# A convolution by two-step transforms on one core: transfers of 48, 32, 64 and 16 rows, and the spectra in DRAM by frequency, then token

## The chip, the cores and the metric

The kernel runs on one core of one Trainium2 chip. The metric is the device time of one execution in microseconds (us). Three timed runs of the kernel before took 922.99, 924.22 and 924.59 us; the median is 924.22 us. The profile that is read below is one more execution, whose instructions span 914.5 us.

## The reference, cut to what matters

Two blocks follow each other. The first is a causal long convolution of each of 128 channels, over 5696 tokens, in 8 batches, with a filter h of the same length:

```python
Xf = np.fft.rfft(x, n=2*S, axis=1)          # x: (8, 5696, 128)
Hf = np.fft.rfft(h, n=2*S, axis=0)          # h: (5696, 128)
y  = np.fft.irfft(Xf * Hf[None], n=2*S, axis=1)[:, :S, :]
```

The second takes y as 45568 tokens of 128 numbers and is a mixture of experts with soft slots (phi: 128 x 32):

```python
logits = y @ phi                            # (45568, 32)
d = softmax(logits, over tokens)            # dispatch
slots = d.T @ y                             # 32 x 128, through 8 small networks w1, relu, w2
c = softmax(logits, over slots)             # combine
out = c @ slot_out                          # (45568, 128)
```

Everything is float32.

## The kernel before, in words

The tokens are laid out as a grid of R1 = 89 rows by N2 = 64 columns. A transform of length N = N1 N2 = 90 x 64 with half-shifted frequencies does the convolution in two steps: one over the rows (90 frequencies, of which pairs are kept as two halves of NP = 45), one over the columns (64). Between the steps the data has to change which index lies on the 128 partitions, and that is done by way of DRAM. So there are three stages, joined by two arrays in DRAM, `f` (the spectra after the first step) and `z` (the products after the second step, turned back over the columns):

- **Stage A** works on a *chunk*: CH = 4 columns and their 4 mirror columns of one input (the filter is input 0, the batches are 1 to 8; 8 chunks each, 72 in all). `load_x` brings the chunk into one of three tiles `xc`, rows on partitions. Before, it is two DMAs, of 80 rows and of 9 rows, to partitions 20 to 108 (`X0 = 20`), each row being two runs of 2 KB (L190). `fold` adds or subtracts the mirror columns on GpSimd (POOL, L201). `stage_a` multiplies by the table `s1` on TensorE (PE, L212), ScalarE (ACT) copies the two results into a tile `fst` (L214), and two DMAs (L218) store it: one for each half `a` of the frequencies, 45 rows each, from partitions 6 to 50 and 82 to 126 (`F0, F1 = 6, 82`). This happens twice a chunk (`comp`), so that a chunk has four stores of `f`.
- **Stage B** works on a *unit* of four frequencies of one input (12 units an input; the twelfth has one frequency). `load_g` loads it into one of three tiles `gt` (L236), now with the columns of both halves on 128 partitions. `stage_b1` multiplies by `wt` on PE (L250) and by the filter's spectrum on VectorE (DVE, L268 and L277); `stage_b2` multiplies by `vt` on PE (L292), ACT copies (L297), and one DMA stores `z` in runs of 1 KB (L300).
- **Stage C** works on a *pair* of chunks of `z`. `load_pair` (L328) loads it with 90 frequencies on partitions, as two DMAs given by `z_blocks`: 64 rows to partitions 32 to 95, and 26 rows to partitions 0 to 25, 16 KB a row. `stage_c1` multiplies by the table `i1` on PE (L347), and the rest turns the result and runs the softmaxes and the dispatch.

In DRAM, before, `f` of an input has the shape (2, 64, 45, 2, 128): half, column, frequency, real or imaginary, channel. A store of `f` therefore writes 4 runs of 1 KB from each of its 45 rows. A load of a unit reads, for each of 128 rows (half, column), one run of 4 KB, since four frequencies lie side by side.

Rows of a tile that no transfer writes are still read by the matmuls, which take all 128 partitions; so the kernel clears the three `xc` tiles and the `zc` tile on DVE at the start (L177, L314). In the tail a second tile `zd` takes the place of released memory, and its gap (partitions 26 to 31) is copied from `zc` by a DMA (L657) ahead of its first load.

The order of the work is written out by hand: a loop over steps t issues one chunk of stage A, one or two units of stage B behind it (1.5 on average), and every second step one pair of stage C. Nearly all DMAs are issued by SyncE (SP), one after another in program order. DMAs take turns on eight completion semaphores, and a DMA waits, on SP, until the one eight DMAs earlier has landed. So at most eight are under way, and a DMA that waits on SP holds all later ones. The buffers are: three `xc`, two folded `x`, five `fst`, three `gt` (loaded two units ahead), three `zst`.

Of the kernel before, what the change touches and what calls it, by code (L numbers as in the profile page):

```python
# [10 lines left out]
F32 = mybir.dt.float32  # L11
# [5 lines left out]

def z_blocks(n):

    return [(0, 64, 32), (64, n - 64, 0)]  # L20


def transform_tables(S, N1, N2, CH, X0, F0, F1):

    N, R1, HALF, P = N1 * N2, S // N2, N2 // 2, 2 * N2
    k1 = np.arange(N1)
    alpha = np.pi * (k1 + 0.5) / N1
    m1 = np.arange(R1) - (N1 - 1) / 2
    a1 = np.outer(m1, alpha)  # L40
    s1 = np.stack([np.cos(a1), -np.sin(a1), -np.cos(a1)], 1)
    a0 = np.outer(alpha, np.arange(N1 // 2) + 0.5)
    i1 = np.stack([np.cos(a0), -np.sin(a0), -np.cos(a0)], 1)
    NP = N1 // 2
    part = s1
    s1 = np.zeros((P, 3, P))
    for a, p in enumerate((F0, F1)):
        s1[X0:X0 + R1, :, p:p + NP] = part[:, :, a * NP:(a + 1) * NP]
    part = i1[np.arange(N1).reshape(2, NP).T.reshape(-1)]
    i1 = np.zeros((P, 3, N2))  # L50
    for r, n, p in z_blocks(N1):
        i1[p:p + n, :, 0:NP] = part[r:r + n]
    k2 = np.arange(N2)
    omega = np.pi * (k1[:, None] + 2 * N1 * k2[None] + 0.5) / N
    m2 = np.arange(HALF) - (N2 - 1) / 2
    a2 = m2[None, :, None] * omega[:, None, :]
    w = np.concatenate([np.cos(a2), np.sin(a2)], 1)
    back = np.arange(N2).reshape(2, HALF // CH, CH).transpose(1, 0, 2).reshape(-1)
    NU = (NP + 1) // 2
    turn = (N1 - 1) / 2 * alpha[:, None] + (N2 - 1) / 2 * omega  # L60
    wq = np.zeros((2, N2, NP, N2))
    vq = np.zeros((2, N2, NU, 2, N2))
    tn = np.zeros((2, N2, 2, (NU + 1) // 2, 2, 2))
    for a in range(2):
# [10 lines left out]
def kernel(  # L75
# [40 lines left out]
    HP = P // 2  # L116
    NQ = NJ // 2
    assert S == R1 * N2 and R1 == N1 - 1 and D == P and CH == Q == 4
    SPLIT = R1 // 16 * 16
    X0, F0, F1 = 20, 6, 82  # L120
    ctx.enter_context(tc.manual_schedule())

    t_s1, t_i1, t_w, t_v, t_turn = [
        nc.inline_tensor(t, f"tab_{n}").ap()
        for n, t in zip(("s1", "i1", "w", "v", "turn"), transform_tables(S, N1, N2, CH, X0, F0, F1))]
    fd = [nc.dram_tensor(f"f_{g}", (2, N2, NP, 2, D), F32, kind="Internal").ap() for g in range(B + 1)]
    zd = [nc.dram_tensor(f"z_{b}", (NP, 2 * N2, 2, D), F32, kind="Internal").ap() for b in range(B)]
    cd = nc.dram_tensor("c_t", (P, B * NQ, Q, 2, MH), F32, kind="Internal").ap()

# [43 lines left out]
    xs = {}  # L173
    xf = [apool.tile([P, CH, D], F32, name=f"x{i}", tag=f"x{i}", bufs=1) for i in range(2)]
    xcs = [apool.tile([P, 2, CH, D], F32, name=f"xc{i}", tag=f"xc{i}", bufs=1) for i in range(3)]
    for t_ in xcs:
        nc.vector.memset(t_[:, :, :, :], 0.0)  # L177

    def load_x(c):
        if c >= (B + 1) * NJ:  # L180
            return
        g, j = divmod(c, NJ)
        src = (h if g == 0 else x[g - 1]).rearrange("(a n) d -> a n d", n=N2)
        t_ = xcs[c % len(xcs)]
        gap = N2 - CH * (2 * j + 1)
        for r in (slice(0, SPLIT), slice(SPLIT, R1)):
            v = src[r, CH * j:CH * (j + 1), :]
            v = bass.AP(tensor=v.tensor, offset=v.offset,
                        ap=[v.ap[0], [gap * D, 2], [1, CH * D]])
            nc.sync.dma_start(  # L190
                out=t_[X0 + r.start:X0 + r.stop, :, :, :].rearrange("p s n d -> p s (n d)"), in_=v)
        xs[c] = t_

    folded = {}
# [1 line left out]
    def fold(c, comp):  # L196
        if c not in xs:
            return
        t_ = xs.pop(c) if comp else xs[c]
        y_ = xf[comp]  # L200
        nc.gpsimd.tensor_tensor(out=y_[:, :, :], in0=t_[:, 0, :, :], in1=t_[:, 1, ::-1, :],  # L201
                                op=AL.subtract if comp else AL.add)
        folded[(c, comp)] = y_

    def stage_a(c, comp):
        g, j = divmod(c, NJ)
        src = folded.pop((c, comp))
        tab = (0, 1) if comp == 0 else (1, 2)
        st = apool.tile([P, CH, 2, D], F32, name="fst", tag="fst", bufs=5)
        for G in range(2):  # L210
            p = bank()
            nc.tensor.matmul(p[:, :], s1[:, tab[G], :],  # L212
                             src[:, :, :].rearrange("p n d -> p (n d)"), start=True, stop=True)
            nc.scalar.activation(st[:, :, G, :],  # L214
                                 p[:, :].rearrange("p (n d) -> p n d", d=D), AF.Copy)
        n0 = comp * HALF + CH * j
        for a, p in enumerate((F0, F1)):
            nc.sync.dma_start(  # L218
                out=fd[g][a, n0:n0 + CH, :, :, :].rearrange("n q c d -> q n (c d)"),
                in_=st[p:p + NP, :, :, :].rearrange("k n c d -> k n (c d)"))  # L220


    gs, prods = {}, {}
# [6 lines left out]
    def load_g(u):  # L230
        if u >= (B + 1) * NW:
            return
        g, w, us = parts(u)
        n = sum(k for _, k in us)
        t_ = bpool.tile([P, 4, 2, D], F32, name="gt", tag="gt", bufs=3)
        nc.sync.dma_start(  # L236
            out=t_[:, 0:n, :, :].rearrange("p q c d -> p (q c d)"),
            in_=fd[g].rearrange("a r q c d -> (a r) (q c d)")[:, 8 * w * D:(8 * w + 2 * n) * D])
        gs[u] = t_

    def stage_b1(u, share):
# [62 lines left out]


    zs, ys, Ls, ds = {}, {}, {}, {}
    zn = used = None
    ybufs = [ypool.tile([P, Q * CH, D + 1], F32, name=f"y{i}") for i in range(2)]
    zring = [ypool.tile([P, 2, 2, CH, 2, D], F32, name="zc")]
    lt = ypool.tile([P, CH, 2, HP], F32, name="lt")  # L310
    dt = ypool.tile([P, CH, 2, HP], F32, name="dt")
    om, op = [ypool.tile([P, CH, D], F32, name=n) for n in ("om", "op")]
    yt = ypool.tile([D, Q * CH, 2, MH], F32, name="yt")
    nc.vector.memset(zring[0][:, :, :, :, :, :], 0.0)  # L314
    for t_ in (lt, dt):
        nc.vector.memset(t_[:, :, :, :], 0.0)
    for t_ in ybufs:
# [15 lines left out]

    def stage_c1(T, between):
        t_ = zs.pop(T)
        kr = used if t_ is zn else P
        y_ = ybufs.pop(0)
        ybufs.append(y_)

        def part(v, f):  # L340
            k = (2 * v + f) * CH
            return y_[:, k:k + CH, 0:D] if f == 0 else y_[:, k + CH - 1:k - 1:-1, 0:D]

        def product(o, tab, q):
            p = bank()
            for h_ in range(2):
                nc.tensor.matmul(p[h_ * HP:(h_ + 1) * HP, :], i1[0:kr, tab, :],  # L347
                                 t_[0:kr, h_, o, :, q, :], start=True, stop=True)
# [212 lines left out]
    for t in range(last_front + 1):  # L561
# [82 lines left out]
        if NA < t <= NA + E:  # L644
# [2 lines left out]


    T = V + 1
    (_, n0, p0), (_, n1, p1) = z_blocks(N1)  # L650
    gap, used = slice(p1 + n1, p0), p0 + n0
# [5 lines left out]
    nc.sync.dma_start(out=zn[gap, :, :, :, :, :].rearrange("k h o n c d -> k (h o n c d)"),  # L657
                      in_=zring[0][gap, :, :, :, :, :].rearrange("k h o n c d -> k (h o n c d)"))
    zring.insert(0, zn)
    load_pair(V + 2)  # L660
    nc.sync.dma_start(out=w1s[:, E - 1, :], in_=moe_w1[E - 1])
# [74 lines left out]
    p = bank()  # L736
# [127 lines left out]
```

## Time and profile before

| what | busy us of 914.5 | share |
|---|---|---|
| TensorE matmuls (PE) | 812.2 | 89% |
| VectorE (DVE) | 645.8 | 71% |
| ScalarE (ACT) | 481.1 | 53% |
| GpSimd (POOL) | 405.2 | 44% |
| the main DMA queue, mean of 16 engines | | 91.7% |

The core moves 272.43 MB, 142.86 MB read from and 128.21 MB written to its memory. The transfers concerned are:

| transfer | line | count | KB each |
|---|---|---|---|
| f <- fst | L218 | 288 | 180 |
| gt <- f | L236 | 99 and 9 | 512 and 128 |
| xc <- x, h | L190 | 72 and 72 | 320 and 36 |
| z <- zst | L300 | 88 and 8 | 512 and 128 |
| zc, zd <- z | L328 | 32 and 32 | 1024 and 416 |

How to read the profile: a group of instructions is named by its line in the kernel, its engine, its operation and the tiles it writes and reads. A wait is given as engine, line and tile, then an arrow, then who ended it; the numbers after it are us in total, how often, and the longest. PEld is TensorE's loading of weights; SPq, PEq and so on are the sequencers that issue. In the strips of 40 digits each digit is a slice of the span, in tenths busy. PEclk, and the number after POOL's in a table by stages, is the share of TensorE's clock that was granted. Beside the groups there are records of every DMA packet, with its start, its duration and its size, but not its direction.

### The profile page before, as it was taken

To read this page: it belongs to the slowest core of one execution; us is meant where nothing else is said; L and a number is where in the kernel's file an instruction comes from. 1 tells how busy PE (TensorE), PEld (TensorE's weight loads), DVE (VectorE), ACT (ScalarE), POOL (GpSimd) and SP (SyncE) were. 2 spreads that over 40 slices of the span, in tenths; PEclk is the share of its full clock that TensorE was granted. 3 is DMA by queue.
4 is the path that set the end of the run, shared out by engine and by line. 5 is a ranking of instruction groups with operands and counts; after the bars stand their busy time and mean duration, and the time that the engine had idled before them with its cause. 6 is when DMAs were issued, how large, how long until landed. Compare 5 with 4: busy or idle time off the path is not lost.

```text
span 914.5 us, 19226 instructions
## 1 busy us (share of the span) xinstructions
PE 812.2 (89%) x7220; PEld 425.9 (47%) x7220; DVE 645.8 (71%) x928; ACT 481.1 (53%) x888; POOL 405.2 (44%) x385
## 2 busy tenths in 40 slices
PE   6968888799999999999999999999988776978893
PEld 2323344344454444544555445444444443345783
DVE  3058767667888878877888777868888885774552
ACT  4624445456556565655666565555654344474442
POOL 4624333245555555555555555555533432472000
PEclk9989999999999999999999999999999998788865
DMA  9999899999999999999999999989989998751798
GB/s 302 269 282 310 256 326 347 292 323 340 285 324 331 304 281 323 320 329 280 329 323 317 289 317 313 311 281 325 334 266 338 305 295 206 223 220 74 281 404 340
DMA packets 156550, 272.43 MB, mean 298 GB/s; under 512 B 11766, under 2 KB 114422, under 8 KB 153317
## 3 DMA queue, kind: packets, MB, share of 16 engines
q1 hardware_dynamic: 155883, 270.85, 91.7%
q8 instruction: 58, 0.95, 0.4%
q10 hardware_dynamic: 576, 0.36, 0.2%
q14 instruction: 33, 0.27, 0.1%
HBM read 142.86 MB, written 128.21 MB: 296 GB/s over the span
## 4 chain that ended last, share of the span: by engine, by line
PE 61%; DMA 27%; issue 4%; ACT 2%; DVE 2%; POOL 2%; SPq 1%; DVEq 0%; POOLq 0%; ACTq 0%
PE bank L212 19%; PE bank L347 10%; PE bt L250 9%; DMA zc<-z 8%; PE bz L292 7%; DMA gt<-f 6%; DMA out_dram<-o 4%; PE bank L375 3%; PE bank L460 3%; DMA zd<-z 3%; DMA z<-zst 2%; DMA f<-fst 2%; PE bank L384 2%; PE bank L436 2%; PE op L817 1%
## 5 line engine op out<-in xcount | busy, mean ns | idle before, releaser
L201 POOL TENSOR_TENSOR x<-xc 128x512 f32<-128x512 f32 x144 | 183.1, 1273 | 260.5 <-PE bank L212 156.9
L212 PE MATMUL bank<-x,s 128*128 128x512 f32 x576 | 273.9, 611 | 9.7 <-POOL x L201 9.6
L214 ACT ACTIVATE fst<-bank 128x512 f32<-128x512 f32 x288 | 171.8, 597 | 94.7 <-PE bank L212 88.3
L297 ACT ACTIVATE zst<-bz 128x1024 f32<-128x1024 f32 x96 | 93.2, 971 | 195.2 <-PE bz L292 191.5
L268 DVE TENSOR_TENSOR p<-bt,Hi 128x1024 f32<-128x1024 f32 x96 | 113.0, 1177 | 107.3 <-PE bt L250 107.1
L212 PEld LDWEIGHTS bank<-x,s 128*128 128x128 f32 x576 | 102.1, 192 | 126.9 <-issue 94.1
L250 PE MATMUL bt<-gt,wt 64*64 64x256 f32 x1620 | 117.4, 397 | 40.0 <-DMA gt<-f 19.8
L347 PE MATMUL bank<-zc,i 128*64 128x512 f32 x480 | 118.0, 614 | 8.5 <-DMA zc<-z 6.2
L277 DVE TENSOR_TENSOR yf<-bt,p 128x512 f32<-128x512 f32 x192 | 119.4, 663 | 3.3
L268 DVE TENSOR_TENSOR bt<-bt,Hr 128x1024 f32<-128x1024 f32 x96 | 113.0, 1178 | 0.0
L250 PEld LDWEIGHTS bt<-gt,wt 64*64 64x64 f32 x1620 | 55.9, 134 | 117.0 <-issue 61.7
L292 PE MATMUL bz<-yf,vt 64*64 64x256 f32 x1440 | 103.7, 386 | 0.0
L366 POOL TENSOR_TENSOR y<-y,op 128x512 f32<-128x512 f32 x64 | 77.4, 1209 | 11.8 <-DVE op L352 9.1
L292 PEld LDWEIGHTS bz<-yf,vt 64*64 64x64 f32 x1440 | 61.8, 136 | 21.1
L366 POOL TENSOR_TENSOR y<-y,om 128x512 f32<-128x512 f32 x54 | 64.0, 1185 | 2.1
L347 PEld LDWEIGHTS bank<-zc,i 128*64 128x64 f32 x480 | 30.9, 138 | 70.3 <-issue 47.4
L375 PE MATMUL bank<-ident,y 109*128 109x109 f32 x512 | 57.5, 268 | 0.7 <-DVE y L366 0.7
L375 PEld LDWEIGHTS bank<-ident,y 109*128 109x128 f32 x512 | 51.2, 146 | 12.9 <-POOL L L449 6.2
L421 POOL MEMSET dt<- 64x8 f32 x32 | 3.4, 106 | 115.9 <-issue 69.2
L377 ACT ACTIVATE yt<-bank 128x360 f32<-128x360 f32 x128 | 50.2, 483 | 2.1 <-PE bank L375 2.1
L817 PE MATMUL op<-so,cT 32*128 32x128 f32 x704 | 46.2, 369 | 4.3 <-ACT o L826 3.4
L268 DVE TENSOR_TENSOR p<-bt,turn 128x1024 f32<-128x1024 f32 (+1 forms) x12 | 14.1, 1176 | 50.7 <-PE bt L250 50.6
(97 smaller groups left out, 861.5 us busy)
## 6 DMA issues: line engine op xcount, KB each, us to landing
f<-fst SPq DMA_DIRECT2D x288, 180.0 KB
gt<-f SPq DMA_DIRECT2D x99, 512.0 KB
z<-zst SPq DMA_DIRECT2D x88, 512.0 KB
zc<-z SPq DMA_DIRECT2D x30, 1024.0 KB
xc<-in_x_dram SPq DMA_DIRECT2D x64, 320.0 KB
out_dram<-o SPq DMA_DIRECT2D x16, 1024.0 KB
zc<-z SPq DMA_DIRECT2D x30, 416.0 KB
out_dram<-o SPq DMA_DIRECT2D x8, 768.0 KB
```

Source lines behind the costliest of these rows:

```text
L201: nc.gpsimd.tensor_tensor(out=y_[:, :, :], in0=t_[:, 0, :, :], in1=t_[:, 1, ::-1, :], op=AL.subtract if comp else AL.add)
L212: nc.tensor.matmul(p[:, :], s1[:, tab[G], :], src[:, :, :].rearrange("p n d -> p (n d)"), start=True, stop=True)
L214: nc.scalar.activation(st[:, :, G, :], p[:, :].rearrange("p (n d) -> p n d", d=D), AF.Copy)
L250: nc.tensor.matmul(bt[q * HP:(q + 1) * HP, a, o, :], wt[r, 2 * i + q, :], t_[r, 2 * o + q, :, :].rearrange("p c d -> p (c d)"), start=True ...
L268: nc.vector.tensor_tensor(out=p_, in0=pv, in1=h_, op=AL.mult)
L277: eng.tensor_tensor(out=y_[r, 0:k, c, :], in0=pv[:, :, c, :], in1=pi[r, 0:k, 1 - c, :], op=op_)
L292: nc.tensor.matmul(bz[a * HP:(a + 1) * HP, q, o, :], vt[r, i, a, :], y_[r, a * m + o, :, :].rearrange("p c d -> p (c d)"), start=True, sto ...
L297: nc.scalar.activation(st[:, 0:m, 0:n, :].rearrange("p o q x -> p q o x"), bz[:, 0:n, 0:m, :], AF.Copy)
L347: nc.tensor.matmul(p[h_ * HP:(h_ + 1) * HP, :], i1[0:kr, tab, :], t_[0:kr, h_, o, :, q, :], start=True, stop=True)
L366: eng.tensor_tensor(out=part_, in0=part(v, 0), in1=o_[:, :, :], op=sign)
L375: nc.tensor.transpose(p[:, i * TR:(i + 1) * TR], ys[T][0:TR, k * CH + i, 0:D], ident[0:TR, 0:TR])
L817: nc.tensor.matmul(pq[q][:, k * D:(k + 1) * D], cT[rows, b, r0:r0 + RW, :] if k < n else cL[rows, :, :], so4[rows, :], start=True, stop=True)
```

## The change

The change redraws three transfers so that each has a number of rows that is a multiple of 16, and turns two dimensions of `f` round.

- **x:** three DMAs in place of two: rows 0 to 63 to partitions 32 to 95; rows 64 to 79 to the even partitions 0 to 30; rows 73 to 88 to the odd partitions 1 to 31. Seven rows are loaded twice, and the table `s1` has zeros for the second copy.
- **f stores:** 48 rows for 45 (from partitions 8 and 72; three rows of each are unused). `f` has the shape (48, 2, 64, 2, 128): frequency, half, column, real or imaginary, channel. A row is then one run of 4 KB, and neighbouring rows lie 128 KiB apart.
- **gt loads:** each of the 128 rows reads four runs of 1 KB, one for each frequency.
- **z loads:** the second block is rows 58 to 89, 32 rows to partitions 0 to 31; six rows come twice, with zeros in `i1`.
- With that, 96 partitions (`KR`) are always written: fold and matmuls take 96, and the clears of `xc` and `zc` and the gap copy into `zd` are gone.

It is for [...]longer runs on the storing side.

```diff
-    return [(0, 64, 32), (64, n - 64, 0)]
+    return [(0, 64, 32), (n - 32, 32, 0)]
+def x_blocks(n):
+    return [(0, 64, 32, 1), (64, 16, 0, 2), (n - 16, 16, 1, 2)]
...
-    X0, F0, F1 = 20, 6, 82
+    F0, F1 = 8, 72
+    QR = 48
+    KR = 96
...
-    fd = [nc.dram_tensor(f"f_{g}", (2, N2, NP, 2, D), F32, kind="Internal").ap() for g in range(B + 1)]
+    fd = [nc.dram_tensor(f"f_{g}", (QR, 2, N2, 2, D), F32, kind="Internal").ap() for g in range(B + 1)]
...
-    for t_ in xcs:
-        nc.vector.memset(t_[:, :, :, :], 0.0)
...
-        for r in (slice(0, SPLIT), slice(SPLIT, R1)):
-            v = src[r, CH * j:CH * (j + 1), :]
+        for r, n, p, step in x_blocks(R1):
+            v = src[r:r + n, CH * j:CH * (j + 1), :]
...
-                out=t_[X0 + r.start:X0 + r.stop, :, :, :].rearrange("p s n d -> p s (n d)"), in_=v)
+                out=t_[p:p + (n - 1) * step + 1:step, :, :, :].rearrange("p s n d -> p s (n d)"), in_=v)
...
-                out=fd[g][a, n0:n0 + CH, :, :, :].rearrange("n q c d -> q n (c d)"),
-                in_=st[p:p + NP, :, :, :].rearrange("k n c d -> k n (c d)"))
+                out=fd[g][:, a, n0:n0 + CH, :, :].rearrange("q n c d -> q (n c d)"),
+                in_=st[p:p + QR, :, :, :].rearrange("k n c d -> k (n c d)"))
...
-            out=t_[:, 0:n, :, :].rearrange("p q c d -> p (q c d)"),
-            in_=fd[g].rearrange("a r q c d -> (a r) (q c d)")[:, 8 * w * D:(8 * w + 2 * n) * D])
+            out=t_[:, 0:n, :, :].rearrange("p q c d -> p q (c d)"),
+            in_=fd[g][4 * w:4 * w + n, :, :, :, :].rearrange("q a r c d -> (a r) q (c d)"))
...
-    nc.vector.memset(zring[0][:, :, :, :, :, :], 0.0)
...
-                nc.tensor.matmul(p[h_ * HP:(h_ + 1) * HP, :], i1[0:kr, tab, :],
-                                 t_[0:kr, h_, o, :, q, :], start=True, stop=True)
+                nc.tensor.matmul(p[h_ * HP:(h_ + 1) * HP, :], i1[0:KR, tab, :],
+                                 t_[0:KR, h_, o, :, q, :], start=True, stop=True)
...
-    nc.sync.dma_start(out=zn[gap, :, :, :, :, :].rearrange("k h o n c d -> k (h o n c d)"),
-                      in_=zring[0][gap, :, :, :, :, :].rearrange("k h o n c d -> k (h o n c d)"))
```

More of the change, by code (lines that the diff above doesn't have):

```diff
@@ L18, in z_blocks, with transform_tables @@
 def z_blocks(n):
-    return [(0, 64, 32), (64, n - 64, 0)]
-def transform_tables(S, N1, N2, CH, X0, F0, F1):
+    return [(0, 64, 32), (n - 32, 32, 0)]
+def x_blocks(n):
+    return [(0, 64, 32, 1), (64, 16, 0, 2), (n - 16, 16, 1, 2)]
+def transform_tables(S, N1, N2, CH, F0, F1):
     N, R1, HALF, P = N1 * N2, S // N2, N2 // 2, 2 * N2
@@ L47, in transform_tables @@
     for a, p in enumerate((F0, F1)):
-        s1[X0:X0 + R1, :, p:p + NP] = part[:, :, a * NP:(a + 1) * NP]
+        done = 0
+        for r, n, p0, step in x_blocks(R1):
+            for i in range(n):
+                if r + i >= done:
+                    s1[p0 + i * step, :, p:p + NP] = part[r + i, :, a * NP:(a + 1) * NP]
+            done = max(done, r + n)
     part = i1[np.arange(N1).reshape(2, NP).T.reshape(-1)]
     i1 = np.zeros((P, 3, N2))
+    done = 0
     for r, n, p in z_blocks(N1):
-        i1[p:p + n, :, 0:NP] = part[r:r + n]
+        i1[p + done - r if r < done else p:p + n, :, 0:NP] = part[max(r, done):r + n]
+        done = r + n
     k2 = np.arange(N2)
@@ L118 @@
     assert S == R1 * N2 and R1 == N1 - 1 and D == P and CH == Q == 4
-    SPLIT = R1 // 16 * 16
-    X0, F0, F1 = 20, 6, 82
+    F0, F1 = 8, 72
+    QR = 48
+    KR = 96
     ctx.enter_context(tc.manual_schedule())
@@ L124 @@
         nc.inline_tensor(t, f"tab_{n}").ap()
-        for n, t in zip(("s1", "i1", "w", "v", "turn"), transform_tables(S, N1, N2, CH, X0, F0, F1))]
-    fd = [nc.dram_tensor(f"f_{g}", (2, N2, NP, 2, D), F32, kind="Internal").ap() for g in range(B + 1)]
+        for n, t in zip(("s1", "i1", "w", "v", "turn"), transform_tables(S, N1, N2, CH, F0, F1))]
+    fd = [nc.dram_tensor(f"f_{g}", (QR, 2, N2, 2, D), F32, kind="Internal").ap() for g in range(B + 1)]
     zd = [nc.dram_tensor(f"z_{b}", (NP, 2 * N2, 2, D), F32, kind="Internal").ap() for b in range(B)]
@@ L200, in fold @@
         y_ = xf[comp]
-        nc.gpsimd.tensor_tensor(out=y_[:, :, :], in0=t_[:, 0, :, :], in1=t_[:, 1, ::-1, :],
+        nc.gpsimd.tensor_tensor(out=y_[0:KR, :, :], in0=t_[0:KR, 0, :, :], in1=t_[0:KR, 1, ::-1, :],
                                 op=AL.subtract if comp else AL.add)
@@ L211, in stage_a @@
             p = bank()
-            nc.tensor.matmul(p[:, :], s1[:, tab[G], :],
-                             src[:, :, :].rearrange("p n d -> p (n d)"), start=True, stop=True)
+            nc.tensor.matmul(p[:, :], s1[0:KR, tab[G], :],
+                             src[0:KR, :, :].rearrange("p n d -> p (n d)"), start=True, stop=True)
             nc.scalar.activation(st[:, :, G, :],
@@ L306 @@
     zs, ys, Ls, ds = {}, {}, {}, {}
-    zn = used = None
+    zn = None
     ybufs = [ypool.tile([P, Q * CH, D + 1], F32, name=f"y{i}") for i in range(2)]
@@ L335, in stage_c1 @@
         t_ = zs.pop(T)
-        kr = used if t_ is zn else P
         y_ = ybufs.pop(0)
@@ L649 @@
     T = V + 1
-    (_, n0, p0), (_, n1, p1) = z_blocks(N1)
-    gap, used = slice(p1 + n1, p0), p0 + n0
     front.close()
```

## The prediction

> **What bounds the kernel now.** I read the page's slices first, then a table of busy time by stage, then the waits by stage, and the timeline only at the two ends.
>
> ```profile
> PE   6968888799999999999999999999988776978893
> ...
> DMA  9999899999999999999999999989989998751798
> DMA packets 156550, 272.43 MB, mean 298 GB/s; under 512 B 11766, under 2 KB 114422, under 8 KB 153317
> ```
>
> TensorE (PE) and the transfers are both at 9 in the middle, so the middle has two bounds. The stages (length, then busy us of PE, PEld, DVE, ACT, POOL, granted clock, DMA share, GB/s) tell where each matters:
>
> ```profile
> 30.00:48.00 18.00, 14.13 (x31) 5.19 (x29) 0.00 (x0) 9.57 (x17) 10.81 (x9) 1.00 0.91 265
> 48.00:170.00 122.00, 101.85 (x692) 46.17 (x692) 87.71 (x100) 51.81 (x80) 42.63 (x35) 0.96 0.95 304
> 170.00:300.00 130.00, 125.12 (x1077) 61.43 (x1077) 99.93 (x138) 73.92 (x131) 67.47 (x62) 0.99 0.99 318
> 300.00:620.00 320.00, 310.73 (x2756) 156.86 (x2754) 252.42 (x363) 190.00 (x348) 170.30 (x158) 1.00 0.98 308
> 620.00:680.00 60.00, 58.51 (x564) 30.02 (x559) 50.40 (x74) 36.07 (x66) 30.61 (x29) 1.00 0.99 320
> ...
> 757.00:797.00 40.00, 30.86 (x210) 13.42 (x207) 24.05 (x41) 17.58 (x42) 15.76 (x19) 0.82 0.83 220
> ```
>
> From 170 to 680 PE works 494.4 of 510 us: no transfer can give back more than 16 us there. From 48 to 170 it idles 20 us at a DMA share of 0.95. The waits say for what (PE 48 to 170, PE 170 to 680, POOL 30 to 48):
>
> ```profile
> PE bt L250 <- DMA gt<-f: 14.5, 5, 6.9
> ...
> PEld bt L250 <- DMA gt<-f: 7.7, 1, 7.7
> ```
> ```profile
> PE bank L347 <- DMA zc<-z: 6.2, 7, 2.3
> PE bt L250 <- DMA gt<-f: 4.8, 7, 1.4
> ```
> ```profile
> POOL x L201 <- DMA xc<-in_x_dram: 3.2, 2, 2.0
> POOL x L201 <- DMA xc<-in_h_dram: 2.6, 2, 1.8
> ```
>
> Early on, spectrum loads (gt) hold PE; later only 11 us of PE's waits are for transfers. At the ends, the DVE clears of xc stand before the first x load, and the gap copy zd<-zc before the first load into zd:
>
> ```profile
> 1.02 0.91 DVE L177 MEMSET xc<- 128x1024 f32 x1 [1.02 <-PEq L850]
> ...
> 1.97 2.87 SPq L190 DMA_DIRECT2D xc<-in_h_dram  x6
> ```
> ```profile
> 759.85 0.80 SPq L657 DMA_DIRECT2D zd<-zc  x1
> 760.70 2.25 SPq L328 DMA_DIRECT2D zd<-z  x2
> ```
> ```profile
> 775.59 3.68 PE L347 MATMUL bank<-zd,i 96*64 96x512 f32 x8 [5.92 <-DMA zd<-z]
> ```
>
> The trace's packet records (size and time of each) give prices: 1 KB takes 46 ns at the median and 48.9 in the mean (49.8 from 48 to 170), 2 KB 84 and 101.9, 4 KB 159 and 201.4 (209 from 48 to 170), 16 KB 625 and 855. So 4 KB cost 184 ns in four pieces and 159 in one, before stalls. The 1 KB ones are nearly all stores, which hardly stall; the loads stall by about a quarter (4 KB: 201/159 = 1.27; 2 KB: 1.21).
>
> [...] The new stores put their rows 128 KiB apart. In the trace the z loads read rows 64 KiB apart at 611 to 625 ns for 16 KB, undisturbed, and the z stores step 128 KiB between a row's four runs at 46 ns a run.
> [...]
>
> **The change, part by part.** A step is one chunk of four columns (about 10.8 us in the middle): four f stores, 1.5 gt loads, one x load, and 1.5 z stores.
>
> [...] bytes grow by 6.7% for f and z and 7.9% for x. I cost this at nothing[...].
>
> *f stores* (4 KB for 4 x 1 KB). An engine's share falls from 12 x 49.8 = 598 ns to 3 x 159 = 477, or 3 x 172 if stretched like before (49.8/46). Taken: 500, so 4 x -98 = -0.40 us a step.
>
> *gt loads* (1 KB for 4 KB). Before: 8 x 209 = 1672 ns an engine in stage 48 to 170. After: 32 packets of p ns. Nothing in the trace shows 32 such loads in a row; the lower end is 46 (the nine 128 KB loads, 1 KB a row, stream at 46), the upper 46 x 1.5 = 69, the 2 KB loads' stretch in the middle (128/84). I take p = 56, about the 4 KB stretch: 1792, so 1.5 x +120 = +0.18 us. At 46 it is -0.30, at 69 +0.80.
>
> *x loads*: three DMAs for two. On the SP queue a DMA more costs 0.40 us of issue and takes another of the eight completion semaphores, on which SP waits in turn: the ninth DMA waits for the first. Behind it on SP stand the f stores and gt loads, and PE waits for these. [...] Taken: zero; ends -0.2 and +0.3 us a step.
>
> A step in sum: -0.40 + 0.18 = -0.22 us of the busiest engine's time, ends -0.9 and +0.7.
>
> *Where it lies on the path.* Start: without clears, x is issued when SP is free, near 0.75 instead of 1.97: -1.2 us; the first fold waited for that load. 30 to 48: about four chunks, with 3.9 us of PE idle; f packets average 54 ns in this stretch, so stores fall by 4 x (12 x 54 - 3 x 187) = 0.35 us a chunk or more: -2 (ends 0, -3). 48 to 170: 15 steps x -0.22 = -3.3, of which I count -2 (ends +9, -10). 170 to 680: PE hides nearly all of 47 steps; -1 (ends +15 if the loads then set the pace, -8 if most of the 11 us of waits go). Tail: the gap copy goes; it held SP 0.85 us, and its six 16 KB packets took 1.3 to 2.45 us ahead of the zd load[...]; PE waited 5.92 us for that load: -2.5. Ends: -0.85, and -6, since PE's matmuls took 1.06 us for 0.59 after that wait (the granted clock had dropped) and a short wait might not drop it. The narrower folds and matmuls (96 rows for 128) cost the same: the trace has 592 ns for both heights of L347's matmuls, and POOL is idle half the time; the zc clear lay beside the fill. After 797 nothing changes.
>
> Sum: -1.2 - 2 - 2 - 1 - 2.5 = -8.7, so 915.5 us.
>
> **The rivals.**
> - *Slow 1 KB loads* (p near 69[...]): -1.2 - 2 + 9 + 15 - 2.5 = +18, so 942 us. For it: DMA shares of 0.98 leave no room, and loads stall where stores don't. Against: the few 1 KB loads seen stream at 46.
> - *Hidden*: the third x DMA eats the early gain and PE hides the rest: -1.2 - 0.85 + 1 = -1, so 923 us. For it: PE at 97% in the middle, SP without a pause from 16 to 48. Against: the tail's copy is plainly on the path.
> - *Transfers were the bound*: -1.2 - 3 - 10 - 8 - 6 = -28, so 896 us. For it: the DMA share. Against: PE has only 11 us of such waits after 170.
>
> **How the numbers follow.** Forecast 0.50, slow loads 0.22, hidden 0.16, large gain 0.12. Part of "hidden" is still over 0.2% faster, and a mild case of slow loads (p near 62) ends between: faster 0.62, same 0.13, slower 0.25. The range leaves out the far halves of the two outer cases: 899 to 935.
>
> **What would show it.** Right: 4 KB stores near 160 ns, 1 KB loads at 50 to 60 ns, the first PE matmul near 6.7 us, PE's first zd wait near 3 us, PE busy 97% from 170 to 680. Wrong: PE waits on gt growing past 48 us, 1 KB packets over 65 ns, SP waiting longer for DMA landings ahead of gt, x loads landing later than before.

## The result, and the profile after

The changed kernel takes 976.92 us (median of 4 runs, 974.08 to 981.88), beside 924.40 us for the kernel before on the same chip. The ratio is 1.056 [1.050, 1.062]: slower by 5.6%, where the forecast was 1% faster and its range ended at 935. The ratios here and below compare, for each kernel, only the executions within 1.5% of its fastest. The profiled execution spans 975.4 us, where that of the kernel before spans 914.5. This last one is a short one: it took 916.4 us, 8 us under the median, so spans and stages set beside it show differences that can be too large by as much.

The slices of the span and the line on packets, as shown before for the old kernel:

```profile
PE   6868888889999889899899889988988787976883
...
DMA  8889999999989998999899989998998998962598
DMA packets 159715, 281.09 MB, mean 288 GB/s; under 512 B 13800, under 2 KB 115304, under 8 KB 156296
```

The whole middle is thinner on both strips: neither PE nor the transfers became the only bound. The table by stage (length, busy us of PE, PEld, DVE, ACT, POOL, granted clock, DMA share, GB/s) says it in numbers:

```profile
30.00:48.00 18.00, 14.10 (x31) 5.28 (x30) 0.00 (x0) 9.55 (x16) 9.00 (x8) 1.00 0.84 250
48.00:170.00 122.00, 98.37 (x607) 44.30 (x608) 78.18 (x88) 44.91 (x70) 38.90 (x32) 0.89 0.91 288
170.00:300.00 130.00, 117.48 (x914) 55.31 (x916) 86.15 (x119) 64.69 (x112) 56.91 (x52) 0.93 0.94 292
300.00:620.00 320.00, 292.43 (x2504) 147.79 (x2497) 223.18 (x328) 172.57 (x315) 156.89 (x146) 0.97 0.94 291
620.00:680.00 60.00, 53.85 (x470) 27.88 (x468) 38.67 (x60) 32.45 (x61) 29.05 (x28) 0.97 0.94 294
```

From 170 to 680 us PE works 463.8 us of 510 (494.4 before), and the DMA share falls (0.98 to 0.94 in the longest stage) at fewer GB/s (291 for 308). If slow packets alone were the cause, one would expect the share to rise. That it falls points to transfers that are *started* too late. PE's waits from 170 to 680 us (total us, times, longest):

```profile
PE bank L356 <- DMA zc<-z: 19.2, 13, 3.1
PE bt L261 <- DMA gt<-f: 16.5, 15, 1.8
```

Before, the same two were 6.2 and 4.8. What holds the transfers back is in the waits of the SP queue in that stretch, first of the kernel before, then of the kernel after:

```profile
SPq L236 <- DMA zc<-z: 51.8, 15, 4.7
...
SPq L300 <- DMA zc<-z: 24.6, 17, 2.3
```
```profile
SPq L229 <- DMA zc<-z: 61.7, 16, 5.4
SPq L247 <- DMA zc<-z: 25.5, 15, 3.6
```

Neither an f store nor a gt load has anything to do with zc. They wait because completion semaphores are taken in turn: each must wait for the DMA eight places earlier, here a z load. (In the trace of the kernel after, of SP's 835 DMAs that have one eight places before them, 833 name the same semaphore as that one, and at most eight DMAs are under way at a time.) Before, the two z loads held a gt load (L236) and a z store (L300); with one DMA more in between, they hold an f store (L229) and the gt load behind it (L247). The totals are alike (76 and 87 us), but the later DMAs stand one place further back. The SP timeline of the kernel after shows one such case (start, length, line, DMA, how many):

```profile
402.67 1.98 SPq L338 DMA_DIRECT2D zc<-z  x2
404.74 1.98 SPq L201 DMA_DIRECT2D xc<-in_x_dram  x3
406.82 6.71 SPq L229 DMA_DIRECT2D f<-fst  x4
415.41 0.38 SPq L247 DMA_DIRECT2D gt<-f  x1
```

Counted from the first z load, the fourth f store is the ninth DMA and the gt load the tenth. The first z load landed at 413.21 by its semaphore, and the store was issued at 413.23; the second landed at 415.35, and the gt load followed at 415.41.

Ahead of stage C there are no z loads, yet time is lost there too. In the SP timeline of the kernel after, between 20 and 30 us, and then of the kernel before, one sees stage A alone:

```profile
23.37 2.03 SPq L201 DMA_DIRECT2D xc<-in_h_dram  x3
25.50 2.26 SPq L229 DMA_DIRECT2D f<-fst  x4
27.86 2.08 SPq L201 DMA_DIRECT2D xc<-in_h_dram  x3
```
```profile
21.24 1.10 SPq L190 DMA_DIRECT2D xc<-in_h_dram  x2
22.43 2.48 SPq L218 DMA_DIRECT2D f<-fst  x4
25.01 1.75 SPq L190 DMA_DIRECT2D xc<-in_h_dram  x2
```

From this chunk to the next it is 4.5 us after and 3.8 before, with SP issuing almost without a gap, about 0.58 us a DMA. Taken over whole chunks between 21 and 44 us, SP issues in 89% of the time before, at 4.0 us a chunk, and in 90% after, at 4.7 us a chunk. (Over 16 to 44 us it is 85% before and 83% after.) So SP's issuing was about full in both, and the longer list takes longer. Waits of SP for landings, by which the limit of eight DMAs under way would show, are small in these 28 us: 0.9 us in all before and 1.7 after.

It isn't the count alone: the new x loads also take SP longer each. These are the x loads issued in the first 10 us, where little else is under way, before and then after (duration in ns, least/median/most):

```profile
L190 SPq DMA_DIRECT2D xc<-in_h_dram x6: 312/362/395, 2.0 to 4.5; - x6
L201 SPq DMA_DIRECT2D xc<-in_h_dram x9: 577/593/762, 0.7 to 6.6; - x9
```

Over all 72 chunks the issuing of stage A's DMAs takes SP 3.50 us a chunk before and 4.57 after.

The tail did become shorter. The table below puts the loss in order of time (us). It gives the time from the first fold of one chunk to that of another, and from the start of the last matmul of stage B to the end; "DMAs" are those of stage A per chunk. Each row is one profiled execution. How far such figures differ by chance can be read where two kernels are the same program up to the point: x_split and split_early have 48.2 and 45.5 from chunk 4 to 12, and x_split and split_swap, which differ only from about 185 us on, have 125.7 and 119.0 from 12 to 28.

| kernel | DMAs | chunk 4 to 12 | 12 to 28 | 28 to 71 | tail |
|---|---|---|---|---|---|
| before | 6 | 42.1 | 117.7 | 471.6 | 157.5 |
| after | 7 | 48.8 | 126.8 | 521.8 | 147.5 |
| x_three | 7 | 49.4 | 125.5 | 506.5 | 161.0 |
| x_split | 7 | 48.2 | 125.7 | 502.3 | 154.8 |
| split_early | 7, then 6 | 45.5 | 124.2 | 473.1 | 158.6 |
| split_swap | 7 | 47.4 | 119.0 | 491.6 | 160.8 |
| f_turned | 6 | 41.7 | 117.6 | 480.4 | 156.3 |
| z_only | 6 | 43.5 | 121.2 | 485.1 | 147.5 |
| after_one | 5 | 42.8 | 115.1 | 475.0 | 148.5 |
| f_one | 4 | 39.0 | 115.4 | 463.0 | 158.5 |

### The profile page after: what moved, and what is told of

It is laid out like the page before. It is cut to its first block, busy times and chain, and to the rows that moved or that the text cites. A ratio compares the mean times of both kernels' runs of the same rounds, so it can differ in the third digit from the quotient of the medians.

```text
span 975.4 us, 19314 instructions
## 1 busy us (share of the span) xinstructions
PE 834.9 (86%) x7220; PEld 435.7 (45%) x7220; DVE 627.6 (64%) x924; ACT 481.0 (49%) x888; POOL 404.8 (42%) x385
## 4 chain that ended last, share of the span: by engine, by line
PE 44%; DMA 41%; issue 4%; ACT 4%; SPq 2%; DVE 2%; POOL 1%; DVEq 0%; ACTq 0%; POOLq 0%
DMA zc<-z 19%; PE bank L223 15%; DMA gt<-f 10%; PE bank L356 8%; PE bt L261 7%; PE bz L303 5%; DMA out_dram<-o 4%; DMA z<-zst 3%; PE bank L445 2%; PE bank L469 2%; PE bank L384 1%; DMA xc<-in_h_dram 1%; PE bank L422 1%; PE bank L393 1%; DMA cl<-c_t 1%
## 5 line engine op out<-in xcount | busy, mean ns | idle before, releaser
L212 POOL TENSOR_TENSOR x<-xc 96x512 f32<-96x512 f32 x144 | 182.3, 1268 | 322.2 <-PE bank L223 184.6
L223 PE MATMUL bank<-x,s 96*128 96x512 f32 x576 | 281.6, 625 | 12.6 <-POOL x L212 12.6
L261 PE MATMUL bt<-gt,wt 64*64 64x256 f32 x1620 | 122.4, 411 | 58.2 <-DMA gt<-f 37.5
L223 PEld LDWEIGHTS bank<-x,s 96*128 96x128 f32 x576 | 105.2, 198 | 135.3 <-issue 99.1
L356 PE MATMUL bank<-zc,i 96*64 96x512 f32 x480 | 126.2, 650 | 29.0 <-DMA zc<-z 22.1
L261 PEld LDWEIGHTS bt<-gt,wt 64*64 64x64 f32 x1620 | 58.8, 138 | 137.9 <-issue 61.4
L303 PE MATMUL bz<-yf,vt 64*64 64x256 f32 x1440 | 109.1, 398 | 0.0
L375 POOL TENSOR_TENSOR y<-y,op 128x512 f32<-128x512 f32 x64 | 77.3, 1208 | 13.5 <-DVE op L361 10.4
L303 PEld LDWEIGHTS bz<-yf,vt 64*64 64x64 f32 x1440 | 65.8, 140 | 21.5 <-issue 1.6
L356 PEld LDWEIGHTS bank<-zc,i 96*64 96x64 f32 x480 | 33.0, 143 | 93.4 <-issue 60.4
```

Source lines behind the costliest of these rows:

```text
L212: nc.gpsimd.tensor_tensor(out=y_[0:KR, :, :], in0=t_[0:KR, 0, :, :], in1=t_[0:KR, 1, ::-1, :], op=AL.subtract if comp else AL.add)
L223: nc.tensor.matmul(p[:, :], s1[0:KR, tab[G], :], src[0:KR, :, :].rearrange("p n d -> p (n d)"), start=True, stop=True)
L261: nc.tensor.matmul(bt[q * HP:(q + 1) * HP, a, o, :], wt[r, 2 * i + q, :], t_[r, 2 * o + q, :, :].rearrange("p c d -> p (c d)"), start=True ...
L303: nc.tensor.matmul(bz[a * HP:(a + 1) * HP, q, o, :], vt[r, i, a, :], y_[r, a * m + o, :, :].rearrange("p c d -> p (c d)"), start=True, sto ...
L356: nc.tensor.matmul(p[h_ * HP:(h_ + 1) * HP, :], i1[0:KR, tab, :], t_[0:KR, h_, o, :, q, :], start=True, stop=True)
```

## The experiments

My theory after this reading was A: the one DMA more in a chunk. Its rival B was the turned layout of f, with 1 KB loads. Further letters are explained where the expectations use them; C, that the places of its rows make the x load lopsided, was my guess, which no trace showed. Times are medians, each beside a median of the kernel before on the same chip; ratios have 95% intervals. The ratio and the medians can differ by a per cent or more where a kernel's times spread widely.

### Which part of the change costs

**x_three**: the kernel before with the x part alone (three loads, of 64, 16 and 16 rows, 96 partitions, no clears of xc).

```diff
-        for r in (slice(0, SPLIT), slice(SPLIT, R1)):
+        for r, n, p, step in x_blocks(R1):
```

> The kernel before with the x part of the change alone (three DMAs a chunk, 96 rows in fold and matmul, no clears of xc). Theory A (one DMA more a chunk, with eight completion semaphores in turn, puts a later f store and the gt load behind the landing of the zc load): most of the loss is here, ratio to before 1.03 to 1.06. Theory B (loads of 1 KB pieces are slow): nothing lost, 0.995 to 1.002. Theory C ([...]the x load is lopsided): a part of the loss, 1.01 to 1.03.

Measured: 980.51 us beside 924.07, ratio 1.059 [1.051, 1.067]. The x part alone makes the whole loss.

**x_split**: nothing but a cut of the 80-row load in two. Same bytes, same rows, same partitions.

```diff
-        for r in (slice(0, SPLIT), slice(SPLIT, R1)):
+        for r in (slice(0, 64), slice(64, SPLIT), slice(SPLIT, R1)):
```

> The kernel before with its 80-row x load cut in two, 64 and 16 rows, to the same places: same bytes, same rows, one DMA more. Theory A: as slow as the x part alone, ratio 1.03 to 1.06. Theories B and C: no change, 0.998 to 1.004.

Measured: 965.15 us beside 924.07, ratio 1.045 [1.036, 1.054]. One DMA more, with no byte more, costs 4.5%. Theories B and C said no change here. The issuing of stage A's DMAs takes SP 4.36 us a chunk, for 3.50 before. Its PE waits from 170 to 680 us are close to those of the changed kernel:

```profile
PE bank L347 <- DMA zc<-z: 17.9, 13, 2.5
PE bt L250 <- DMA gt<-f: 16.4, 15, 3.2
```

**f_turned**: the kernel before with the f part alone (48 rows, layout by frequency, 4 KB stores, 1 KB loads).

```diff
-                out=fd[g][a, n0:n0 + CH, :, :, :].rearrange("n q c d -> q n (c d)"),
+                out=fd[g][:, a, n0:n0 + CH, :, :].rearrange("q n c d -> q (n c d)"),
```

> The kernel before with the f part alone (48 rows, stores in runs of 4 KB, loads in pieces of 1 KB), x and z as they were. Theory A: no loss, ratio 0.99 to 1.003, as the number and order of DMAs is that of before. Theory B: most of the loss, 1.03 to 1.06, and 1 KB packets with a mean over 52 ns. Theory C: no loss.

Measured: 926.71 us beside 924.07, ratio 1.003 [1.000, 1.006]. B falls: the layout neither costs nor brings anything that counts. Its profiled execution (span 922.3 us) has PE waiting 12.2 us for z and 7.8 for gt from 170 to 680 us, so waits of that size go with an unchanged time.

**after_x_two**: the changed kernel with two x loads, of 64 and 32 rows.

```diff
-    return [(0, 64, 32, 1), (64, 16, 0, 2), (n - 16, 16, 1, 2)]
+    return [(0, 64, 32, 1), (n - 32, 32, 0, 1)]
```

> The changed kernel with x in two DMAs, 64 and 32 rows (rows 57 to 88 to partitions 0 to 31), all else as changed. Theory A: the loss is gone, ratio to before 0.985 to 1.003. Theory B: still slow, 1.04 to 1.06. Theory C: still slow, 1.04 to 1.06[...].

Measured: 935.23 us (917.82 to 941.02) beside 924.07. The medians differ by 1.2%, where the change differs by 5.6%: most of the loss goes with the third DMA. The spread of the four executions is too wide for a ratio.

### Is it the turn of the semaphores?

The next kernels exchange two calls in a step, so that the x loads are issued ahead of the z loads. The DMA that comes eight places after a z load is then another one.

```diff
+        if t < NA:
+            load_x(t + 3)
         if pair(-2) is not None:
             load_pair(pair(-2))
-        if t < NA:
-            load_x(t + 3)
```

**split_swap** (x_split with the exchange):

> The kernel before with its 80-row x load cut in two (as in the run before), and in the loop the x load issued ahead of the pair load of z, so that no f store, gt load or z store is the eighth DMA after a z load. Same number of DMAs, same bytes. Theory A1 (the loss is the wait on the semaphore of the DMA eight back, where that is a z load of 9 to 12 us): ratio to before 0.99 to 1.015, against 1.045 for the cut alone. Theory A2 (the loss is SP's issue time for 72 DMAs more, or any DMA more being dear in itself): 1.04 to 1.05 as without the exchange.

Measured: 942.60 us beside 926.88, ratio 1.014 [1.007, 1.021], where x_split had 1.045. Its PE waits from 170 to 680 us:

```profile
PE bank L347 <- DMA zc<-z: 18.9, 8, 4.3
PE bt L250 <- DMA gt<-f: 4.2, 5, 1.8
```

The waits for gt are back at the size of before (4.2 for 4.8), those for zc, now issued later, are not. In the table the exchange changes nothing from chunk 4 to 12, where no z load exists (47.4 for 48.2), and from 28 to 71 it is 11 us shorter (in the longest of the four executions). The 7 us from 12 to 28 mostly can't be due to the exchange: the first z load comes at about 185 us, up to which both kernels are the same program, and at chunk 20 split_swap is already 5 us ahead (127.1 for 132.1 us).

**after_swap** (the whole change with the exchange):

> The changed kernel, whole, with the same exchange (x load ahead of the pair load of z). A1: most of the loss goes, ratio to before 0.99 to 1.02 (against 1.056). A2: 1.045 to 1.06.

Measured: 949.15 us (933.03 to 955.13) beside 926.88, ratio 1.013 [1.004, 1.022], from two of four executions; the medians differ by 2.4%.

**before_swap** (the kernel before with the exchange):

> The kernel before with the exchange alone. There the gt load is the eighth DMA after a z load and waits for it on SP. A1: a little faster, ratio 0.98 to 1.0. A2: no change, 0.998 to 1.003.

Measured: 918.90 us beside 926.88, ratio 0.993 [0.989, 0.996]. So the exchange by itself is worth 0.75%, and the comparison has to be made with it on both sides: 942.60/918.90 is 1.026, and the two ratios to before, unrounded, give 1.022. The extra DMA costs 4.5% in the one order and 2.2 to 2.6% in the other. So the order, and with it the place where the turns fall, is about two fifths to a half of the loss, not all of it.

**after_two_swap** (the whole change, two x loads, exchange):

> The changed kernel with x in two DMAs (64 and 32 rows) and the exchange. A1: the best of all, ratio to before 0.97 to 0.995, as the clears and the gap copy are gone and no gt load stands behind a z load. A2: like the two-DMA version without the exchange, 1.0 to 1.02.

Measured: 925.02 us beside 926.88, with times from 903.67 to 1160.61. The ratio, 0.979 [0.973, 0.984], rests on two of 22 executions and the medians differ by 0.2%, so no difference can be read from this.

### The part ahead of stage C, and the tail

**split_swap_act**: split_swap, with every second f store of the first 24 chunks issued by ACT, to take issue time off SP.

```diff
-            nc.sync.dma_start(
+            (nc.scalar if a and c < 3 * NJ else nc.sync).dma_start(
```

> The kernel before with the 80-row x load cut in two and the exchange (ratio 1.014 before this edit), and for the first 24 chunks the second store of each pair of f stores issued by ACT, which makes the data, not by SP. Same DMAs, same bytes, same turns on the eight semaphores; SP issues 5 DMAs a chunk early on, not 7. Theory A3 (what is left of the loss lies ahead of stage C, where SP issues DMAs without a pause and each takes it about 0.6 us): chunk 8's first fold at 37 to 40 us (43.5 without the edit, 38.6 in the kernel before), ratio 0.995 to 1.008. Theory A4 (what is left there is the limit of eight DMAs under way): chunk 8's fold stays at 43 to 44 us, ratio 1.01 to 1.02.

Measured: 973.62 us beside 926.64, ratio 1.054 [1.046, 1.062], and chunk 8 begins at 52.1 us, later than in any other kernel. Neither theory said this. The stores of both engines take turns on the same semaphores (in the trace of the kernel before, where ACT issues four DMAs, all 768 that have one eight places before them name the same semaphore as that one), and SP now waits for f stores to land: from 8 to 52 us 15.3 us with f stores and 8.1 us with x loads, 11.2 us in one case, where split_swap has no such wait. What SP was to save in issuing it lost in waiting. The edit changes two things at once and doesn't decide on issue time.

**z_only**: the kernel before with the z part alone (second z load of 32 rows, no gap copy, no clear of zc).

```diff
-    return [(0, 64, 32), (64, n - 64, 0)]
+    return [(0, 64, 32), (n - 32, 32, 0)]
```

> The kernel before with the z part of the change alone (second block of 32 rows to partitions 0 to 31, 96 rows in the matmuls, no clear of zc, no gap copy into zd). Theory: the tail's gap copy with what it drags along ([...]PE waiting for zd at a lower clock) is worth 7 to 10 us from the last stage-B matmul to the end (157.5 us before, 147.5 us in the changed kernel), and the middle is as before: ratio 0.988 to 0.996. Rival (the six rows more[...] slow the z loads in the middle): the tail's gain is given back, 0.998 to 1.01.

Measured: 929.18 us beside 926.64, ratio 1.001 [0.997, 1.004]. The tail is 10 us shorter, as in the change. From chunk 28 to 71 it is 13.5 us longer, and PE's waits from 170 to 680 us are up from 6.2 and 4.8:

```profile
PE bank L348 <- DMA zc<-z: 10.1, 11, 2.1
PE bt L253 <- DMA gt<-f: 8.6, 10, 1.5
```

The tail gains and the whole doesn't, so the rest must give it back; how much of it the middle does is not sure. Up to 8 of the 13.5 us are due to the short execution of the kernel before, and the waits are no larger than those of f_turned, which has the z loads of before.

**z_swap** (z part and exchange):

> The z part alone with the exchange of x load and pair load: should hold both gains, ratio 0.98 to 0.99 (0.9925 for the exchange alone). If the longer z loads now hold up x loads or c_t stores behind them: 0.99 to 1.0.

Measured: 921.55 us beside 926.64, ratio 0.986 [0.981, 0.990], under both kernels; by the medians it is 0.5% under the kernel before.

**z_swap_act** (z_swap with the ACT edit):

> The same with the second store of each pair of f stores on ACT for the first 24 chunks. A3 says that SP's issue is a bound in the kernel before too ahead of chunk 8 (3.9 us a chunk for 3.5 of PE): 2 to 6 us less than without, ratio 0.972 to 0.988. A4: no difference, or slower by up to 1% where ACT stands waiting for a semaphore.

Measured: 940.91 us beside 926.64, ratio 1.021 [1.014, 1.027]. The ACT edit costs here too, with only six DMAs a chunk.

**split_early**: the cut of x_split for the first 28 chunks only.

```diff
+        cuts = (0, 64, SPLIT, R1) if c < 28 else (0, SPLIT, R1)
-        for r in (slice(0, SPLIT), slice(SPLIT, R1)):
+        for r in [slice(*k) for k in zip(cuts, cuts[1:])]:
```

> The kernel before, with the 80-row x load cut in 64 and 16 rows for the first 28 chunks only; bytes, rows and everything after chunk 28 as before. In the version with the cut in all chunks, chunk 28's first fold began 17 us later than before (199.3 for 182.4), and the end came 41 us later (965 for 924). If these two stretches are two separate losses, chunk 28 starts at 195 to 201 here and the end keeps that and no more: 936 to 944 us. Rival: what is lost ahead of chunk 28 is made up later by idle time in the middle: 926 to 931.

Measured: 937.61 us beside 927.12, ratio 1.017 [1.007, 1.026]. Chunk 28 begins at 197.4 for 182.4, and from there on the pace is that of the kernel before (473.1 for 471.6). The early loss stays, and it is a quarter (10.5 of 41 us by the medians) to somewhat over a third (1.7 of 4.5% by the ratios) of x_split's.

### The count itself

The last three kernels take DMAs away. The two f stores of half a chunk are joined: with the frequencies of both halves interleaved over the partitions (one half on every second partition from 16, the other from 17), their 96 rows stand 64 KiB apart in the turned layout, and one DMA stores them. Bytes and runs are those of f_turned. The code shown is that of f_one.

```diff
-        s1[X0:X0 + R1, :, p:p + NP] = part[:, :, a * NP:(a + 1) * NP]
+        s1[X0:X0 + R1, :, p:p + 2 * NP:2] = part[:, :, a * NP:(a + 1) * NP]
...
-        for a, p in enumerate((F0, F1)):
-            nc.sync.dma_start(
-                out=fd[g][:, a, n0:n0 + CH, :, :].rearrange("q n c d -> q (n c d)"),
-                in_=st[p:p + QR, :, :, :].rearrange("k n c d -> k (n c d)"))
+        nc.sync.dma_start(
+            out=fd[g].rearrange("q a n c d -> (q a) n c d")[:, n0:n0 + CH, :, :].rearrange("r n c d -> r (n c d)"),
+            in_=st[F0:F0 + 2 * QR, :, :, :].rearrange("k n c d -> k (n c d)"))
```

**after_one**: the whole change, third x load included, with joined stores (five DMAs).

> The whole change, three x loads included, but with the two f stores that follow each other joined into one DMA of 96 rows (the frequencies of the two halves are interleaved over the partitions, so that a row's neighbour in DRAM is 64 KiB away; the same bytes and runs of 4 KB). A chunk then has five DMAs of stage A: three x loads, two f stores; before had six, the change seven. Theory of the count (issue time of SyncE early, turns of the eight semaphores in the middle): at or under the kernel before, 905 to 926 us, chunk 8's first fold at 36 to 39 us, no f store or gt load waiting for z loads more than before. Rival, that the third x load hurts by itself (small loads of 16 rows to every second partition, or where it stands in the order): above 955 us, chunk 8 still at 42 or later.

Measured: 920.20 us beside 927.12, ratio 0.990 [0.986, 0.994]. The loss of 5.6% is gone; what waits on SP for z loads is now z stores (44.0 us from 170 to 680 us) and the stores of c_t (14.9 us), no longer f stores and gt loads. So the third x load does no harm where two stores fewer make room for it: issuing takes SP 3.22 us a chunk here. One detail missed: chunk 8 began at 42.9, not at 36 to 39. About 4.8 us of that came before chunk 4 (27.4 for 22.6), where an x load waited for the landing of a table (2.4 us). From chunk 4 to 12 it only kept the pace of the kernel before, with one DMA less, at a granted clock of 0.88 from 16 to 44 us (1.00 before).

**f_one**: the kernel before with the turned f and joined stores (four DMAs).

> The kernel before with the f part of the change and its f stores joined two by two: four DMAs of stage A a chunk (two x loads, two f stores) for six. If SyncE's issue of about 0.6 us each sets the pace of the chunks ahead of stage C (six took 3.9 us, seven 4.6), chunk 8's first fold starts at 34 to 36.5 us for 38.5 before, chunk 28 at 170 to 178 for 182.4, and the end is 900 to 918 us. Rival: the early pace is set by the transfers' own time (the same bytes): chunk 8 at 37.5 to 39.5, and the end 918 to 928.

Measured: 903.17 us beside 927.12, ratio 0.982 [0.971, 0.992], the fastest of all by its median. Against f_turned, which moves the same bytes in the same runs, the ratios stand 0.982 to 1.003. PE's waits from 170 to 680 us:

```profile
PE bank L347 <- DMA zc<-z: 3.4, 3, 2.0
...
PE bt L250 <- DMA gt<-f: 1.8, 3, 1.1
```

They are down from 11.0 to 5.2 us, and PE works 500.4 of those 510 us. In the early stretch the stage from 16 to 44 us reads so (columns as above):

```profile
16.00:44.00 28.00, 27.77 (x65) 10.80 (x64) 0.00 (x0) 19.30 (x33) 20.36 (x17) 1.00 0.98 334
```

PE is busy for 27.8 of 28 us, with SP issuing in 68% of them. Before, it was 26.2, and in x_split 22.2: the kernel before stood near the edge between the two bounds. Chunk 8 began at 37.0, between what both theories said. From chunk 4 to 12 two DMAs fewer bring 3.1 us, where one more costs 6.1 in x_split, since PE then sets the pace.

**z_swap_one** (z_swap with joined stores):

> The best version so far (the z part of the change, with the x loads issued ahead of the z loads in a step) with the f part and its stores joined two by two. If the count of DMAs is what counts: 5 to 15 us under the 921.5 of that version, 905 to 916. If the count is no bound once it is at six, or the larger stores come back as waits for fst buffers: 918 to 926.

Measured: 918.05 us (900.79 to 931.16) beside 927.12, ratio 0.982 [0.978, 0.986]. The parts don't add up: it isn't faster than f_one, and beside z_swap (0.986) the joined stores bring 0.4 points, within the intervals.

## Why the prediction was wrong

**The step that failed** is the third x DMA: "Taken: zero; ends -0.2 and +0.3 us a step". The step named what happened: 0.40 us more of issue, one more of eight semaphores in turn, the f stores and gt loads queued behind, PE waiting for these. But it called the sum zero, and its ends went into a sum "of the busiest engine's time", that is transfer time, not time on SP's queue. The issue was too small as well: stage A's issuing grew by 0.86 us a chunk in x_split and 1.07 in the changed kernel, and already in the trace of before a DMA took SP 0.62 us in the mean from 170 to 680 us. Measured by x_split, the term is +0.8 us a chunk from chunk 4 to 12 ((48.2 - 42.1)/8), +0.5 from 12 to 28 and +0.7 from 28 to 71 (30.7/43). In the profiled executions these three stretches make 44.8 of the 48.5 us by which x_split's span is longer; by the medians the whole is 41. The single figures are rough, but the groups stand apart: without the two kernels with the ACT edit, the six with seven DMAs a chunk begin chunk 12 at 72.5 to 75.1 us, the seven with six DMAs at 64.7 to 68.8. The term lies above its upper end in every stage, and alone it turns the sign of the sum.

**The bound.** "170 to 680: PE hides nearly all of 47 steps" treated PE's 97% as slack for whatever the queue does. The prediction looked for two bounds, PE and transfer time. There was a third, the issuing on SP, with its order and its time, and the wait lines of SP were not read for it: the 76 us in which SP stood behind z loads were in the profile of before. What they showed was which DMA comes ninth; one more DMA moves that. SP's waiting isn't costly as such (all waits of SP from 170 to 680 us add up to 311 us in f_one and to 233 before); it costs where the DMA held up is needed soon.

**f stores and gt loads.** The packet times were near. How many packets of a transfer fall to the busiest engine was an estimate; it is not shown, since the packet records don't name their engine. 1 KB packets, about half of them loads now, take 52.5 ns in the mean from 170 to 680 us (48.3 before, nearly all stores); if the stores kept their time, the loads take about 57 (an estimate), for 56 taken. 4 KB packets take 179 there, against 159 to 172 taken. f_turned, 1.003, shows both terms together as nothing where the steps gave -0.22 us a chunk (-16 us over 72, of which about -5 were counted).

**More rows.** Taken at nothing. x_three and x_split differ by 1.4 points with overlapping intervals, so this isn't decided for x. For z, z_only hints at a cost, since its shorter tail doesn't shorten the whole; whether the six rows more a pair (26 to 32, to partitions 0 to 31) are the reason, no run tells.

**Start.** -1.2 us was said; the first matmul came at 7.42 for 7.87, so -0.45. (The kernels with the clears of xc begin at 7.8 to 8.4 us, those without at 6.9 to 7.5.)

**Tail.** Right in kind, mis-sized: -2.5 was said, it was -10 (the nine kernels with the z part have tails of 147.0 to 151.7 us, the nine without 154.8 to 161.1). PE no longer waits for the first load into zd, and its clock isn't lowered (granted 1.00 from 838 to 850 us, where the kernel before had 0.50 from 775 to 785): the line that read 3.68 us behind a wait of 5.92 now reads

```profile
840.49 1.94 PE L356 MATMUL bank<-zd,i 96*64 96x512 f32 x8
```

The prediction's further end (-6) named this possibility, and even that was short.

**The rivals.** "Slow 1 KB loads" came nearest by its time (942) for a reason that the runs refute. "Hidden" named the right DMA ("the third x DMA eats the early gain"), and gave it about 1 us where it took over 40. Of the signs listed for wrong, PE's waits for gt and SP's waits for landings came true, and 1 KB packets over 65 ns did not. Of those for right, the packet times came near, but PE was busy 91% from 170 to 680 us, not 97%. A slip without weight: fifteen steps at the ends of -0.9 and +0.7 make -13.5 and +10.5 us, not -10 and +9.

**What stays open.** That one DMA more a chunk causes the loss is shown by x_split, and the joined stores confirm it (after_one and f_one; with the z part and the exchange they bring hardly anything). That the order of issue makes up part of it is shown by the exchange; that it does so by the turns on z loads is read from the waits for gt, which go with it. That the part ahead of stage C is SP's issue time is read from the trace: SP issues in about 90% of the time in both kernels, and the added issue (0.86 us a chunk in x_split, over the whole run) is of the size of the loss (0.7 to 0.8). It is not shown by an experiment of its own: joined stores remove a DMA's issue and its semaphore at once. The limit of eight DMAs under way, theory A4, finds little room in SP's waits there: x_split has a single one for a landing from 16 to 44 us, 3.7 us for a table. Why the new x loads take SP 0.59 us to issue where the old ones took 0.36 is open. Of the 2.2 to 2.6% that is left with the exchange, the first 28 chunks can make 1.1 to 1.7 (split_early); the rest is not split further. PE's own time is also up, 834.9 us for 812.2 with the same 7220 matmuls, at a mean clock of 0.929 for 0.945, and so is x_three's (839.8 us). x_split loses 48.5 us of span with only 6 of this, so it isn't the cause of that loss; of the 12 us by which the changed kernel's span is longer than x_split's, it may be a part.

## What to carry to other kernels

Where one engine issues nearly all DMAs in order and completion semaphores are taken in turn, count the DMAs of a loop step, and find which one stands eight places behind the slowest: one DMA more costs its issue and shifts every later turn, even if it brings no byte more, as in x_split (4.5% for one DMA more in a chunk). So a transfer cut in three to have its rows in multiples of 16 can lose far more than it gains (5.9% lost in x_three), and joining two transfers (by choosing the partition order so that their rows have one pitch in DRAM) can win with no byte less (2 points in f_one, 0.4 and not clear of chance in z_swap_one). Read the queue's own waits before calling a transfer free, even where the compute engine is at 97%.

## What the runs showed of the hardware

- The time that a DMA takes its issuing engine didn't follow its size. Of the nine x loads that the changed kernel issues in its first 10 us, three of 256 KB and six of 64 KB, each held SP for 0.58 to 0.76 us (median 0.59). The six that the kernel before issues there, of 320 and 36 KB, took 0.31 to 0.40 each. Landing follows size a little: over the changed kernel's run the 64 KB loads landed after 4.9 us (median), the 256 KB ones after 6.2.
- Two stores of 48 rows joined into one DMA of 96, with the same bytes in the same runs, brought 2 points: f_one has a ratio of 0.982 to the kernel before, f_turned 1.003. Beside the places of the rows, what changed was the number of DMAs, four of stage A a chunk for six.
- Packets of 1 KB took 48.3 ns in the mean from 170 to 680 us before, when nearly all were stores. With about half of them loads, which fetch 512 pieces of 1 KB in one DMA, the mean over both kinds was 48.4 in f_one, 50.2 in f_turned and 52.5 in the changed kernel. Packets of 4 KB take 179 ns in the mean there in the changed kernel, where they are mostly stores to rows 128 KiB apart, and 202 before, where they were mostly loads.
- The same matmuls of the tail took 1.94 us for eight without a wait ahead (granted clock 1.00), and 3.68 after a wait of 5.92 (granted clock 0.50).
